# Attention and a state-space layer on one core: two PSUM tiles of three banks around one shared bank

## The chip, the cores and the metric

One core of a Trainium2 chip. The time is that of the device in microseconds, as a median over runs of the whole program.

## What is computed

Two independent layers on a sequence of 2048 rows of 640 values, put side by side in the output. Cut to what matters:

```
# A: a diagonal state-space layer
h = Lam_bar * h + (B_bar x)[t]            # 2048 steps, complex, 640 states
y = 2 * Re(C h) + x * Dskip
# B: attention, 32 query heads of 20 values, one shared key and value head
scores = (q @ k.T) * 20 ** -0.5           # 32 heads, 2048 x 2048
p = softmax(scores); o = p @ v
out = concat([y, o @ wo], axis=-1)
```

## The kernel before

A planner written in Python (`Plan`, and the loop in `main`) places every instruction when the program is built. It keeps a clock for each engine, offers at each step all instructions that could come next, and takes the one that can begin first, with biases. The biases and limits come from a random generator (`vary`), whose seed is changed 64 times over the run; `SEEDS` holds the seeds. So the order on each engine is fixed in the program, and an edit of the planner, or of the seeds, moves instructions everywhere.

Attention is worked in 32 groups (4 blocks of 512 queries x 8 groups of 4 heads). A group has 64 units: one head's 512 queries against 128 keys, which is one PSUM bank of 512 float values on 128 partitions. The 2048 units go one of two ways:

- Most are exponentiated by ScalarE (`ex_op`, line 1263). TensorE fills a tile of two or three banks with QK products (`fill_op`; all products are recorded at line 421), and one ScalarE instruction turns the whole tile into bf16 numbers in `P`.
- The others are VectorE's units, called D here. `dx_op` (line 1269) copies a bank of scores as integers into `Pd`, and `sh_op` (line 1274) makes three shifted copies of up to three units at once; the four together, read as bf16, stand for the exponential. A group may have at most 16 (`QUOTA`), and `want_d` decides whether the next fill takes one along.

TensorE then multiplies both kinds with the values (`pv_op`), up to four products at once in the bank `PV`, and VectorE takes the finished group out (`raw_op`, line 1307).

PSUM has eight banks: tile `R0` with three, tile `R1` with two, `PV`, and two banks `B0` and `B1`. Tiles are filled in turn, `R0`, `R1`, `R0`, and so on, and a tile can be filled again once its exp is done. D units use `B0` or `B1`, or the third bank of `R0` (`R0c`), which is then lent and the tile is filled with two units. The list `owner` says who has a bank.

The background work uses `B0` and `B1` too, one bank for each sum: the Q projections, the state-space layer's input products (`scan_in`; line 901 reads 1024 values out of a bank, each twice), its output products (`y_tile`), and the output projection (`proj_ops`). GpSimd does the products between the scans (line 917). At the end `last_ops` uses the free tiles for the last output rows. Where TensorE would be idle for long, the planner puts in products with zeros (`PV<-cs,VP`) to keep its clock up.

`P` holds 25 units as 10 slots, of three and two in turn.

Of the kernel before, what the change touches and what calls it, by code (L numbers as in the profile page):

```python
# [243 lines left out]
class _Kernel:  # L244
    S, D, H, DH = 2048, 640, 32, 20
    NC, NQB, NKC, NGG = 5, 4, 16, 8
    BANKS = 2
    PIECES = "abcd"
    TILES, PTILES, DUNITS, DSHIFT, QRING = (3, 2), 10, 9, 3, 4
    SHIFTS = (0, 33, 65, 95)  # L250

# [13 lines left out]
    SEEDS = (19006, 20002, 21006, 22006, 23001, 24003, 25001, 26002, 27008, 28003, 0, 30006, 31008, 32005, 33006,  # L265
# [28 lines left out]
    def alloc(self):  # L294
        S, NC = self.S, self.NC
        nc = self.nc
        self.R = [self.scope.enter_context(nc.psum_tensor(f"R{i}", [128, 512 * n], FP32))
                  for i, n in enumerate(self.TILES)]
        self.PV = self.scope.enter_context(nc.psum_tensor("PV", [128, 512], FP32))
        self.BB = self.scope.enter_context(nc.psum_tensor("B", [128, 512 * self.BANKS], FP32))  # L300
        self.B = [self.BB[:, 512 * i:512 * i + 512] for i in range(self.BANKS)] + [self.R[0][:, 1024:1536]]
        self.bkeys = [f"B{i}" for i in range(self.BANKS)] + ["R0c"]
        self.p.psum.update(["R0", "R0c", "R1", "R1b", "PV", *(f"B{i}" for i in range(self.BANKS))])
# [25 lines left out]
        self.sb("P", [128, self.PTILES * 5 // 2, 512], BF16)  # L329
# [7 lines left out]
        self.wq_raw = self.P[:].rearrange("p s n -> p (s n)")[:, 18 * 512:18 * 512 + NC * 640].rearrange("p (c n) -> p c n", c=NC)  # L337
# [92 lines left out]
    def setup(self):  # L430
        t, NC, S = self.t, self.NC, self.S
        self.x_keys = [f"xbT{c}" for c in range(NC)] + [f"xbT{NC - 1}b"]
        K = self
# [48 lines left out]
        pk = ["P7", "P8", "P9"]  # L482
# [23 lines left out]
        banks = [(K.R[1], 0, "R1"), (K.R[1], 512, "R1b"), (K.BB, 0, "B0"), (K.BB, 512, "B1")]  # L506
# [39 lines left out]
        for m, src, keys in ((0, K.R[1][:, 0:1024], ["R1", "R1b"]), (1, K.BB[:, 0:1024], ["B0", "B1"])):  # L546
            dve(lambda e, m=m, src=src: e.tensor_reduce(
                out=K.mabs[:, m:m + 1], in_=src, axis=AX.X, op=ALU.max, apply_absolute_value=True),
                keys, [f"mabs{m}"], n=1024)
# [339 lines left out]
    def scan_in(self, ops, dve, b, c):  # L889
        K, NC, prog = self, self.NC, self.prog  # L890
        u = NC * b + c
        xs = [f"xaT{b % 2}_{i}" for i in range(NC)]
        gate = lambda: prog["u"] >= u and prog["x"] >= b
        for k, (nm, BT) in enumerate((("BTre", K.BTre), ("BTim", K.BTim))):
            h = Hold()
            for cd in range(NC):
                ops.append(self.mms([self.m1(lambda h=h: h.T[:, :], BT[:, cd, 128 * c:128 * c + 128],
                                             K.xaT[:, b % 2, cd, :], cd == 0, cd == NC - 1)],
                                    [f"{nm}{i}" for i in range(NC)] + xs, [None], accum=cd > 0, lock=cd == 0,
                                    gate=gate if cd == 0 else None, hold=h))  # L900
            dve(lambda e, k=k, h=h: e.tensor_tensor(  # L901
                K.tm[:, 2 * k:2 * k + 2, :], bass.AP(tensor=K.BB, offset=512 * int(h.key[1]),
                                                       ap=[[512 * self.BANKS, 128], [0, 2], [1, 512]]),
                K.cs[:, c, :, :], ALU.mult), [None, "cosT", "sinT"], [f"tm{2 * k}", f"tm{2 * k + 1}"], 1024, hold=h,
                free=True, done=(lambda: prog.update(a=u + 1)) if k else None)
# [162 lines left out]
    def last_ops(self, gates, normed):  # L1068

        K, NC = self, self.NC  # L1070
        spots = [(K.R[0], 0, 0, 512, self.TILES[0]), (K.R[1], 1, 0, 512, self.TILES[1]), (K.BB, 2, 0, 512, self.BANKS)]
        keys = [["R0"], ["R1"], ["B0", "B1"], ["R0c", "PV"]]
# [40 lines left out]
    def vary(self, seed):  # L1113
# [10 lines left out]
        self.lend = r.choice((0.5, 1.0))  # L1124
        self.open, self.first = r.choice((0.6, 0.7)), r.choice(("sy", "proj", None))

    def main(self):
# [10 lines left out]
        tile_left = {}  # L1138
# [27 lines left out]
        fins = self.last_ops([lambda: done(0), lambda: done(1), lambda: done() and cur["raw"] == NG and not (any(owner[:2]) or sy or norm or proj),  # L1166
# [3 lines left out]
        owner = ["rest", "rest", None]  # L1170
        rest[-1].done = lambda: owner.__setitem__(slice(0, 2), [None, None])
        holds, since = {}, {}

        def bank(o):

            f = [i for i in range(2) if owner[i] is None]
            if not f:
                return None
            return min(f, key=lambda i: p.begin("pe", (), (f"B{i}",)))
# [6 lines left out]
        def pick(size, with_d):  # L1186

            g = next(i for i in range(NG) if taken[i] < 64)
            out, d = [], None
# [7 lines left out]
            if with_d:  # L1197
                gd = d_group(g)
                j = min(range(4), key=lambda j: (dcount[gd][j], made(gd, j), -len(left[gd][j])))
                if left[gd][j]:  # L1200
                    d = (gd, j)
                    heads.add(j)
# [27 lines left out]
        def want_d(g, t, n_tile, lent=False):  # L1230
            if not (g > 0 or taken[g] >= 24) or d_group(g) is None:
                return False
            if dunit_left.get(cur["d"] - self.DUNITS, 0):
                return False
            if lent:
                return (self.lend < 9 and owner[2] is None and t_left() and backlog(t) <= self.backlog - 0.5 * n_tile - self.lend
                        and p.begin("pe", (), ("R0c",)) <= t + self.spared[n_tile])
            if bank(None) is None:
                return False
            if any(owner[:2]) and any(t - x > self.starved[name] * (name != "qt" or len(self.qsent) > 0) for name, x in since.items()):  # L1240
# [4 lines left out]
        def fill_op(n, out, d, x):  # L1245
            lst, reads, writes = [], set(), ([f"R{n % 2}"] if out else []) + ["R0c"] * (len(out) == 3)
            units = list(out) + ([d] if d else [])
            wide = len({j // 2 for _, j in units}) == len(units)
            for i, (g, j) in enumerate(units):
                kc = left[g][j][-1]  # L1250
                lo, n_rows = (64 * (j // 2), 64) if wide else (32 * j, 32)
                dst = K.B[x][:, :] if i == len(out) else K.R[n % 2][:, 512 * i:512 * i + 512]
# [3 lines left out]
            if d:  # L1256
                writes.append(K.bkeys[x])
            return self.mms(lst, sorted(reads), writes, kind="QK")

        def ex_op(n, size):  # L1260
            b = 5 * (n // 2 % (self.PTILES // 2)) + 3 * (n % 2)
            dst = K.P[:, b:b + size, :].rearrange("p a n -> p (a n)")
            return Op("act", lambda e: e.activation(dst, K.R[n % 2][:, 0:512 * size], ACT.Exp, scale=self.exp_scale),  # L1263
                      [f"R{n % 2}"] + ["R0c"] * (size == 3), [f"P{n % self.PTILES}"], occ=act_t(512 * size), lat=0.17)

        def dx_op(n):
            u, x = n % self.DUNITS, holds[n]
            key = K.bkeys[x]
            return Op("dve", lambda e: e.tensor_scalar(K.Pd[:, 0, u, :], K.B[x][:, :], self.d_off, 0.0, op0=ALU.add,  # L1269
                                                       op1=ALU.max), [key], [f"Pd{u}_0"], occ=dve_t(512))  # L1270
# [14 lines left out]
        def pv_op(g):  # L1285
            lst, keys = [], set()
            for j in range(4):
# [3 lines left out]
                if how == "act":  # L1291
                    rhs, w = K.P[:, b, :], 0
                    keys |= {f"P{a}", "VP0"}
# [18 lines left out]
        while True:  # L1312
# [14 lines left out]
            if cur["fill"] < cur["act"] + 2 and any(x < 64 for x in taken) and not early:  # L1327
                n = cur["fill"]
                g = next(i for i in range(NG) if taken[i] < 64)
                if g in qt_done:  # L1330
                    t = p.begin("pe", (), (f"R{n % 2}",))
                    size, x = self.TILES[n % 2] - (n % 2 == 0 and owner[2] is not None), bank(None)
                    d = want_d(g, t, n % 2)
                    if not d and size == 3 and want_d(g, t, 0, True):
                        size, d, x = 2, True, 2
                    out, d = pick(size, d)
# [5 lines left out]
                    if d is None and want_d(g, t, 2):  # L1342
                        d = pick(0, True)[1]
                        if d:
                            offer("fill", fill_op(n, [], d, bank(None)), 0.2, arg=([], d, bank(None)))
            full = bool(tiles) and tile_left.get(tiles[0][0] - self.PTILES, 0) > 0
            if tiles:
                n, out = tiles[0]
                if tile_left.get(n - self.PTILES, 0) == 0:
# [20 lines left out]
            for name, th in threads:  # L1370
# [15 lines left out]
                if o.eng == "pe":  # L1386
                    bias = 0.0 if own else self.wait - 0.1 * (name == self.first)
                elif own:
# [32 lines left out]
            if kind == "bg":  # L1421
                th = dict(threads)[name]
                th.popleft()
                if o.lock:
                    owner[int(o.hold.key[1])] = name
                    since.pop(name, None)
                if o.free:
# [3 lines left out]
            elif kind == "fill":  # L1431
                out, d, x = arg
                self.units += len(out) + (d is not None)
                if out:
                    n = cur["fill"]
                    cur["fill"] += 1
                    tile_left[n] = len(out)
# [3 lines left out]
                if d:  # L1441
                    g, j = d
# [4 lines left out]
                    holds[cur["d"]] = x  # L1447
                    owner[holds[cur["d"]]] = "D"
                    cur["d"] += 1
            elif kind == "ex":  # L1450
                n, out = tiles.popleft()
                cur["act"] += 1
                b = 5 * (n // 2 % (self.PTILES // 2)) + 3 * (n % 2)
                for i, (g, j, kc) in enumerate(out):
                    items[g][j].append(("act", kc, n % self.PTILES, b + i, n))
            elif kind == "dx":
                n, (g, j, kc) = dunits.popleft()
                owner[holds[n]] = None
                u = n % self.DUNITS
                if half and (u == 0 or half[0][1][0] != g):  # L1460
                    shifts.extend((tuple(half), i) for i in range(1, 4))
                    half.clear()
                half.append((u, (g, j, kc)))
                dunit_left[n] = 4
                items[g][j].append(("dve", kc, u, 0, n))
                if len(half) == self.DSHIFT or u == self.DUNITS - 1:
# [6 lines left out]
            elif kind == "pv":  # L1473
                g = cur["pv"]
                for j in range(4):
                    if items[g][j]:
# [3 lines left out]
                        if how == "act":  # L1480
                            tile_left[h] -= 1
# [49 lines left out]
```

## Time and profile before

| | |
|---|---|
| median of 3 runs | 770.23 us (769.33 to 770.93) |
| profiled execution | 770.28 us |
| its span, first to last instruction | 768.6 us |
| mean granted clock of TensorE | 0.989 |
| busy: ScalarE, VectorE, TensorE, GpSimd | 98%, 92%, 92%, 58% |
| exps (line 1263) | 677 instructions, 733.1 us busy |
| copies of D units (line 1269) | 436 instructions, 295.4 us busy |
| shifted copies (line 1274) | 513 instructions, 260.2 us busy |

The busy time of a group is the time that its engine had one of its instructions in work; the mean length of one can overlap the next. "Idle before" is the time that the engine had nothing in work ahead of these instructions, and what ended it. A line such as L421 is that of a helper that records every product, so products are told apart by their tiles.

### The profile page before, as it was taken

To read this page: it belongs to the slowest core of one execution; us is meant where nothing else is said; L and a number is where in the kernel's file an instruction comes from. 1 tells how busy PE (TensorE), PEld (TensorE's weight loads), DVE (VectorE), ACT (ScalarE), POOL (GpSimd) and SP (SyncE) were. 2 spreads that over 40 slices of the span, in tenths; PEclk is the share of its full clock that TensorE was granted. 3 is DMA by queue.
4 is the path that set the end of the run, shared out by engine and by line. 5 is a ranking of instruction groups with operands and counts; after the bars stand their busy time and mean duration, and the time that the engine had idled before them with its cause. 6 is when DMAs were issued, how large, how long until landed. Compare 5 with 4: busy or idle time off the path is not lost.

```text
span 768.6 us, 16664 instructions
## 1 busy us (share of the span) xinstructions
PE 704.8 (92%) x6538; PEld 213.4 (28%) x6538; DVE 708.3 (92%) x1236; ACT 752.5 (98%) x710; POOL 446.0 (58%) x867
## 2 busy tenths in 40 slices
PE   5799988888889999998889999988889999889998
PEld 2222222222222333322223323322223332223333
DVE  5599999999998999999997999999999789999986
ACT  8999999999999999999999999999999999999995
POOL 5612354579989931088997300199986469990040
PEclk9899999899999999999999999999999999999999
DMA  9366301000021100220002100040000201000020
GB/s 186 57 143 134 74 16 49 8 24 14 3 51 30 42 8 27 56 60 15 15 9 67 42 23 9 23 93 10 15 15 28 66 33 34 14 15 17 18 61 35
DMA packets 61179, 31.50 MB, mean 41 GB/s; under 512 B 41510, under 2 KB 61102, under 8 KB 61102
## 3 DMA queue, kind: packets, MB, share of 16 engines
q1 hardware_dynamic: 59606, 30.14, 15.9%
q8 instruction: 52, 0.85, 0.5%
q10 hardware_dynamic: 1496, 0.30, 0.2%
q14 instruction: 25, 0.20, 0.1%
HBM read 9.21 MB, written 12.69 MB: 28 GB/s over the span
## 4 chain that ended last, share of the span: by engine, by line
ACT 74%; PE 15%; DVE 9%; POOL 1%; DMA 1%; issue 1%; ACTq 0%; DVEq 0%; POOLq 0%
ACT P L1263 72%; PE R L421 5%; PE PV L421 5%; PE B L421 4%; DVE Pd L1274 4%; DVE Pd L1269 3%; DVE hh L928 1%; DVE tm L901 1%; POOL tm L858 1%; DMA WO<-in_B_wk_dram 1%; ACT cs L691 1%; ACT Pd L690 0%; ACT KT L538 0%; DVE CGre L860 0%; ACT L503 0%
## 5 line engine op out<-in xcount | busy, mean ns | idle before, releaser
L1263 ACT ACTIVATE P<-R 128x1024 bf16<-128x1024 f32 (+1 forms) x677 | 733.1, 1354 | 4.3 <-PE R L421 1.8
L421 PE MATMUL R<-QT,KT 32*128 32x512 bf16 (+1 forms) x1685 | 266.9, 389 | 48.6 <-ACT P L1263 37.1
L1269 DVE TENSOR_SCALAR Pd<-B 128x512 int16<-128x512 f32 x363 | 245.5, 682 | 19.4 <-PE B L421 17.0
L1274 DVE TENSOR_SCALAR Pd<-Pd 128x1536 int16<-128x1536 int16 (+2 forms) x513 | 260.2, 541 | 0.4
L421 PE MATMUL PV<-Pd,VP 128*32 128x512 bf16 x1744 | 256.9, 386 | 2.0 <-DVE OTr L1307 1.0
L421 PE MATMUL PV<-P,VP 128*32 128x512 bf16 x1612 | 253.3, 389 | 0.7 <-DVE OTr L1307 0.6
L917 POOL TENSOR_TENSOR tm<-hh,cs 128x128 bf16<-128x128 f32 x320 | 163.9, 533 | 17.7 <-DVE hh L928 8.3
L421 PEld LDWEIGHTS R<-QT,KT 32*128 32x128 bf16 (+1 forms) x1685 | 66.1, 91 | 301.0 <-ACT P L1263 271.0
L421 PE MATMUL B<-QT,KT 32*128 32x512 bf16 x363 | 141.0, 389 | 0.0
L917 POOL TENSOR_TENSOR uh<-tm 128x128 bf16<-128x128 bf16 x160 | 81.0, 527 | 97.6 <-DVE tm L901 93.7
L917 POOL TENSOR_TENSOR W<-tm 128x128 bf16<-128x128 bf16 x160 | 93.5, 608 | 49.4 <-PE B L421 45.3
L421 PEld LDWEIGHTS PV<-Pd,VP 128*32 128x32 bf16 x1744 | 60.1, 94 | 65.7 <-issue 40.5
L421 PEld LDWEIGHTS PV<-P,VP 128*32 128x32 bf16 x1612 | 58.1, 94 | 58.8 <-issue 46.6
L1011 POOL TENSOR_TENSOR OTd<-OTd,rwide 128x128 bf16<-128x128 bf16 x80 | 33.2, 443 | 60.0 <-DMA OTd<-o_rows 58.2
L1269 DVE TENSOR_SCALAR Pd<-R 128x512 int16<-128x512 f32 x73 | 49.9, 683 | 3.0 <-PE R L421 2.4
L901 DVE TENSOR_TENSOR tm<-B,cs 128x1024 bf16<-128x1024 f32 x40 | 48.5, 1213 | 1.0 <-PE B L421 0.6
L858 POOL TENSOR_SCALAR tm<-W,sc 128x128 f32<-128x128 bf16 x40 | 32.3, 821 | 27.5 <-DVE CGre L860 15.9
L421 PE MATMUL B<-CGre,W 128*128 128x384 bf16 (+1 forms) x160 | 46.4, 305 | 0.0
L421 PE MATMUL B<-CGim,W 128*128 128x384 bf16 (+1 forms) x160 | 45.5, 299 | 0.0
L928 DVE TENSOR_TENSOR_SCAN hh<-sc,hini,uh 128x512 f32<-128x512 f32 x30 | 40.7, 1358 | 0.0
L421 PEld LDWEIGHTS B<-QT,KT 32*128 32x128 bf16 x363 | 32.9, 91 | 0.0
L421 PE MATMUL B<-xaT,BTre 128*128 128x512 bf16 x100 | 30.1, 384 | 0.1
(149 smaller groups left out, 437.2 us busy)
## 6 DMA issues: line engine op xcount, KB each, us to landing
o_rows<-OTr SPq DMA_DIRECT2D x32, 128.0 KB, 1.7
QT<-q_rows SPq DMA_DIRECT2D x30, 128.0 KB, 2.2
q_rows<-Qd SPq DMA_DIRECT2D x16, 160.0 KB, 2.9
OTd<-o_rows SPq DMA_DIRECT2D x16, 160.0 KB, 3.4
out_dram<-ystage SPq DMA_DIRECT2D x16, 160.0 KB, 1.9
out_dram<-ostage SPq DMA_DIRECT2D x12, 160.0 KB, 1.8
P<-in_B_wq_dram SPq DMA_DIRECT2D x1, 800.0 KB, 5.6
WO<-in_B_wo_dram SPq DMA_DIRECT2D x4, 200.0 KB, 3.4
```

The costliest lines, as they stand in the source:

```text
L421: ins = e.matmul(o() if callable(o) else o, lhsT=l, rhs=r, start=st, stop=sp, skip_group_check=True, **kw)
L691: act(lambda e, c=c, b=b: e.activation(K.cs[:, c, :, :].rearrange("p i n -> p (i n)"), K.tri[:, 4 * b + 2:4 * b + 4, :].rearrange("p r n - ...
L858: pool(lambda e, y=y, c=c, gy=gy, i=i: e.tensor_scalar(K.ctmp[:, i:i + 128], y[:, i:i + 128], sc[:, gy, c:c + 1], None, op0=ALU.mult), key ...
L901: dve(lambda e, k=k, h=h: e.tensor_tensor(K.tm[:, 2 * k:2 * k + 2, :], bass.AP(tensor=K.BB, offset=512 * int(h.key[1]), ap=[[512 * self.BA ...
L917: put(lambda e, c0=c0, end=end: e.tensor_tensor(out[:, c0:end], a[:, c0:end], b[:, c0:end], op), reads, [writes + h], n, gate=None if i el ...
L928: dve(lambda e, ri=ri, ini=ini: e.tensor_tensor_scan(K.hh[:, ri, :], dec, K.uh[:, ri, :], ini, ALU.mult, ALU.add), ["sc", *(f"uh{ri}{h}" f ...
L1011: ops.append(Op("pool", lambda e, c=c, m=m: e.tensor_tensor(K.OTd[:, m, c], K.OTd[:, m, c], K.rwide[:, c], ALU.mult), rw + [f"OTe{dd}" for ...
L1263: return Op("act", lambda e: e.activation(dst, K.R[n % 2][:, 0:512 * size], ACT.Exp, scale=self.exp_scale), [f"R{n % 2}"] + ["R0c"] * (siz ...
L1269: return Op("dve", lambda e: e.tensor_scalar(K.Pd[:, 0, u, :], K.B[x][:, :], self.d_off, 0.0, op0=ALU.add, op1=ALU.max), [key], [f"Pd{u}_0 ...
L1274: return Op("dve", lambda e: e.tensor_scalar(K.Pd[:, i, a:b, :], K.Pd[:, 0, a:b, :], float(self.SHIFTS[i]), 0.0, op0=ALU.subtract, op1=ALU ...
```

## The change

PSUM is cut anew: one tensor `R` of seven banks and `PV`. Tile 0 has banks 0 to 2, bank 3 is the one shared bank `B0`, tile 1 has banks 4 to 6. Either tile can now hold three units, or two and lend its third bank to a D unit: tile 0 lends bank 2, tile 1 bank 4. Both are neighbours of the shared bank. A fill may take two D units along, one in the lent bank and one in the shared bank, and `dx_op` then copies both with one instruction of 1024 values. Background work has the one shared bank where it had two. `P` becomes a ring of 25 single units. `vary` draws some more limits (`prefer`, `pair`, `more`, `gap`), and all seeds are other ones. Cut to its core:

```diff
-    BANKS = 2
+    BANKS = 1
-    TILES, PTILES, DUNITS, DSHIFT, QRING = (3, 2), 10, 9, 3, 4
+    TILE, PUNITS, DUNITS, DSHIFT, QRING = 3, 25, 9, 3, 4
...
-        self.B = [self.BB[:, 512 * i:512 * i + 512] for i in range(self.BANKS)] + [self.R[0][:, 1024:1536]]
+        self.RB = self.scope.enter_context(nc.psum_tensor("R", [128, 512 * (2 * self.TILE + 1)], FP32))
+        self.R = [self.RB[:, 0:1536], self.RB[:, 2048:3584]]
+        self.B = [self.RB[:, a:a + 512] for a in (1536, 1024, 2048)]
+        self.bkeys = ["B0", "R0c", "R1c"]
...
+        self.lend, self.prefer = r.choice((0.0, 0.5, 1.0)), r.choice((False, True))
+        self.pair, self.more = r.choice((True, True, False)), r.choice((0.0, 0.5, 1.0))
+        self.gap = dict(sy=r.choice((0.0, 4.0, 8.0)), proj=r.choice((0.0, 4.0, 8.0)), sa=r.choice((0.0, 0.0, 4.0)),
+                        qt=r.choice((0.0, 0.0, 4.0)))
...
-            f = [i for i in range(2) if owner[i] is None]
...
+            return 0 if owner[0] is None else None
...
         def dx_op(n):
             u, x = n % self.DUNITS, holds[n]
+            if n in pairs:
+                a = 1024 if x == 1 else 1536
+                return Op("dve", lambda e: e.tensor_scalar(K.Pd[:, 0, u:u + 2, :].rearrange("p u n -> p (u n)"), K.RB[:, a:a + 1024],
+                                                           self.d_off, 0.0, op0=ALU.add, op1=ALU.max),
...
-                    size, x = self.TILES[n % 2] - (n % 2 == 0 and owner[2] is not None), bank(None)
-                    d = want_d(g, t, n % 2)
-                    if not d and size == 3 and want_d(g, t, 0, True):
-                        size, d, x = 2, True, 2
+                    lent = 1 + n % 2
+                    size, x = self.TILE - (owner[lent] is not None), [0]
+                    if self.pair and size == 3 and want_d(g, t, 0, lent, True):
+                        size, d, x = 2, 2, [lent, 0] if lent == 1 else [0, lent]
+                    elif (d := want_d(g, t, n % 2)) and not (self.prefer and size == 3 and want_d(g, t, 0, lent)):
+                        d = 1
+                    elif size == 3 and want_d(g, t, 0, lent):
+                        size, d, x = 2, 1, [lent]
```

In the changed kernel the exp stands at line 1276, the copies of D units at lines 1283 and 1286, and the shifted copies follow behind.

151 lines of the change are left out of this document (81 added, 70 removed), and 8 rows, old and new, of the table SEEDS.

## The prediction

> **What bounds the kernel now.** I read the page first: the busy times, then the chain that ended last.
>
> ```profile
> span 768.6 us, 16664 instructions
> ...
> PE 704.8 (92%) x6538; PEld 213.4 (28%) x6538; DVE 708.3 (92%) x1236; ACT 752.5 (98%) x710; POOL 446.0 (58%) x867
> ...
> ACT 74%; PE 15%; DVE 9%; POOL 1%; DMA 1%; issue 1%; ACTq 0%; DVEq 0%; POOLq 0%
> ```
>
> ScalarE is busy 98% and carries 74% of the chain, nearly all of it in the exps of line 1263. Next I read the groups of instructions with shapes kept apart, since the change alters shapes.
>
> ```profile
> L1263 ACT ACTIVATE P<-R 128x1024 bf16<-128x1024 f32 x419 | 457.8, 1189 | 1.1 <-PE R L421 0.7 <-PE B L421 0.2
> L1263 ACT ACTIVATE P<-R 128x1536 bf16<-128x1536 f32 x258 | 418.3, 1621 | 3.2 <-PE R L421 1.2 <-PE B L421 1.1 <-PE PV L421 0.6
> ...
> L1269 DVE TENSOR_SCALAR Pd<-B 128x512 int16<-128x512 f32 x363 | 245.5, 682 | 19.4 <-PE B L421 17.0
> L1274 DVE TENSOR_SCALAR Pd<-Pd 128x1536 int16<-128x1536 int16 x354 | 205.5, 608 | 0.2
> ...
> L901 DVE TENSOR_TENSOR tm<-B,cs 128x1024 bf16<-128x1024 f32 x40 | 48.5, 1213 | 1.0 <-PE B L421 0.6
> ```
>
> There are 677 exps over 419 x 2 + 258 x 3 = 1612 units. The idle column is almost empty, but it misleads: neighbouring exps overlap in the records (457.8 + 418.3 is more than the span), so an exp that starts late looks merely long or short, not preceded by idle time. The starts in the timeline tell more. Where the next tile was ready, starts follow each other after 0.904 us (two banks) or 1.331 us (three banks), medians over the whole run. So a bank costs 0.427 us and an instruction 0.904 - 2 x 0.427 = 0.050 us. At these spacings the exps need 419 x 0.904 + 258 x 1.331 = 722.2 us. From the first start (21.7) to the last end (759.0) they take 737.4. The other 15 us are starts that came late: 14.8 us between starts, 0.3 us in the last exp's own end. Summed by what was running before the late start: after a two-bank exp 12.4 us over 418 (29.6 ns each), after a three-bank exp 2.4 us over 258 (9.4 ns each). A longer exp gives TensorE more time to bring the next tile.
>
> How a late start looks, in the timeline (start, length):
>
> ```profile
> 485.06 2.15 ACT L1263 ACTIVATE P<-R 128x1024 bf16<-128x1024 f32 x2
> ...
> 486.69 0.33 PE L421 MATMUL B<-CGim,W 128*128 128x384 bf16 x1
> 486.70 0.69 DVE L1307 CAST OTr<-PV 128x512 bf16<-128x512 f32 x1 [0.19 <-PE PV L421]
> 486.95 0.39 PE L421 MATMUL R<-QT,KT 32*128 32x512 bf16 x3
> ...
> 487.38 1.02 ACT L1263 ACTIVATE P<-R 128x1024 bf16<-128x1024 f32 x1 [0.17 <-PE R L421]
> ```
>
> TensorE had other products in its order, so the fill came at 486.95 and the exp started 0.43 us after it. Last, the waits and the clock (columns of the second: length, busy us of PE, PEld, DVE, ACT, POOL with counts, PEclk, DMA).
>
> ```profile
> DVE Pd L1269 <- PE B L421: 17.0, 58, 0.7
> ...
> PE R L421 <- DVE Pd L1269: 3.2, 8, 0.8
> ```
>
> ```profile
> 28.00:35.00 7.00, 6.59 (x29) 1.21 (x29) 1.55 (x4) 6.38 (x7) 2.31 (x11) 0.52 0.05 4
> ...
> 141.00:147.00 6.00, 5.97 (x36) 1.12 (x32) 5.17 (x11) 5.33 (x5) 2.42 (x4) 0.50 0.08 26
> ```
>
> TensorE's fills hardly ever wait for VectorE's copies (3.2 us in 8 waits); by the same list they wait for ScalarE 598 times, 271 us. In three short stretches, 17 us in all, the clock is about half: the two shown and 120 to 124 (0.57, ScalarE busy throughout). ScalarE idles 0.62 + 0 + 0.67 = 1.3 us in them.
>
> **The change, part by part.** The counts are those of the instructions in the two built programs; everything else keeps its count.
>
> Exps: 419 -> 387 of two banks, 258 -> 279 of three. That is 11 instructions and one unit less: 387 x 0.904 + 279 x 1.331 = 721.2 us, so **-1.0 us**, all on the bounding engine. [...]
>
> VectorE's units: 436 -> 437. As instructions: 436 -> 391 copies of one bank and 0 -> 23 of two. One bank is spaced at 0.601 us. No copy of two banks is in the trace; the nearest is line 901, also 1024 float values from PSUM, spaced at 1.134. From below it could cost 2 x 0.427 as a pure stream on ScalarE's rate, from above 2 x 0.601. I take 1.134: 23 x 1.134 - 45 x 0.601 = 26.1 - 27.0 = -1.0 us. The shifted copies (1274): +15 of three units (0.469), -30 of two (0.336), -30 of one (0.21), +12 of four, not in the trace (0.60 by the steps of 0.133): 7.0 - 10.1 - 6.3 + 7.2 = -2.1 us. Together -3.1 us of VectorE. This is not on ScalarE's path by itself. In 6 of 15 stretches of 50 us VectorE is busy over 48 us; if its saving is spread evenly, 1.2 us fall there. ScalarE's idle there is small, so I count half: **-0.6 us** (bounds 0 and -3.1).
>
> TensorE: 677 -> 666 fills (0.32 us from the start of one to the next product, read at 102.64) and 881 -> 866 groups of PV products (0.22 us), 3 more warming products: about -6 us of 582. It waits for ScalarE in most fills, so this is worth nothing by itself.
>
> Where the units go is the real change. Before, 363 of VectorE's 436 units lay in the two banks of their own and 73 in the lent third bank of tile 0. After, 365 lie in lent banks of either tile and 72 in the shared bank. So tile 1 gets a third bank, and 574 of 666 fills are three units (318 of 677 before). Late starts, priced by what covers them: 387 x 29.6 + 278 x 9.4 = 14.1 us against 14.8, so **-0.7 us**. This is the price I take, because it follows the mechanism seen in the starts. Two other prices of the same term are rivals below.
>
> Background work now has one bank, where it had two. While VectorE reads that bank, TensorE cannot begin the next background sum, and what is queued behind it on TensorE waits too, if the order puts it too early. I cost it at nothing: VectorE's own units leave the shared bank (363 -> 72), and in the new order the last y products stand at unit 1982 of 2048, before at 2002, so background work doesn't pile up at the end. Without that cover one late background read is 1.2 us (line 901).
>
> Set-up and tail: the same instructions on other banks. First exp at 21.7 and the 9.6 us after the last exp are kept, cost 0; the last fill has 18 PV products behind it where it had 30, but the tail follows the last exp's end. The P ring keeps 25 units, now without holes; exps waited for none, so 0. DMAs and the queues of SP and POOL keep their counts.
>
> Sum: -1.0 - 0.7 - 0.6 = -2.3 us. The profiled execution took 770.28 (span 768.6 and 1.7 around it), the median of the three runs is 770.23. So 768.0. A measurement here can tell 0.2%, 1.5 us, from no change: below 768.7 is faster, above 771.8 slower.
>
> **Rivals.**
>
> No change. Late starts go with the size of the fill before them, not with the cover: per fill of two units 8.9 ns, of three 24.3, of four 29.7. The new mix (21, 574, 71) gives 16.2 us, +1.4, which eats the 1.0 of the exps: 770.7, or 770.1 with VectorE's relief. For it: a fill of three waits for one more bank. Against: size and place go together in this trace.
>
> Slower: the lent bank ties three engines. In the new order 378 fills write a bank that VectorE's copy of two fills earlier has to have left (235 before, 68 of them a lent bank with its unit); if VectorE is late, the whole tile is late and ScalarE with it. Fills that reused a lent bank so soon were followed by 31.5 ns of lateness each, the rest by 19.6, and the 16 that reused a bank after one fill by 92. With 378 x 31.5 + 288 x 19.6 = 17.5 us the exps lose 2.7 more: 770.3 - 1.0 + 2.7 = 772.0. It decides against the change above 27 ns per lent fill (0.378 x 27 + 5.6 = 14.8 + 1.0), and reaches 774 at 37. Against it: before, banks were lent when the others were full, so those fills were late for that reason too.
>
> The pairs are rare and the change does little: 46 of 437 units. That alone is 23 x 0.068 = 1.6 us of VectorE, none of it seen: 770.2, same.
>
> The clock. If TensorE idles a little in every round of the banks, its clock drops more often than three times. Ten more stretches like those three would be 57 us, with 1.3/17 lost in each us: +4.3, so 772.3. [...]
>
> **How the numbers follow.** Forecast 0.46, no change 0.20 and rare pairs 0.04, lent bank 0.24, clock 0.06. So faster 0.46, same 0.24, slower 0.30. The forecast's own range is 765.0 to 768.7: its low end lets half of the late starts fall to the three-bank price ((14.8 - 6.3)/2 = 4.3, and 1.0). The range of 8 in 10 goes from 765.0 to 773.0, over the rivals at 770, 772.0 and 772.3 and part of the lent bank's upper end.
>
> **What would show it.** Right: 387 and 279 exps at the old spacings; the exps' time from first start to last end 735.1; VectorE's pair of banks near 1.13 from start to start; TensorE waiting for line 1286 (the copies) no more than a few us. Wrong: a wait of PE R for VectorE's copies grown from 3.2 towards 10 us with late starts behind it, more than three dips of the clock, or late starts above 17 us in sum.

## The result: slower by 0.3%

The changed kernel takes 771.65 us (median of 20 runs, 770.50 to 776.97), the kernel before 769.80 beside it (20 runs): a ratio of 1.0032 [1.0018, 1.0046]. Timed once more, beside other runs of the kernel before, it was 1.0025 [1.0011, 1.0039]. So it loses 1.9 to 2.5 us where the prediction had it gain 2.3; the forecast was wrong in sign. By the marks that the prediction set from 770.2 (faster below 768.7, slower above 771.8) 771.65 by itself would be no change, and it lies in the range of 8 in 10 (765.0 to 773.0), though outside the forecast's own (765.0 to 768.7). That it is slower shows in the ratio, whose interval leaves out 1.

The profiled execution of the changed kernel took 773.31 us, 1.7 above its own median, so single places of it are not typical; a second profile of the same kernel (772.58 us) and a second one of the kernel before (769.35 us) are read beside it. The second of after is slow too, 1.4 above the median of its own series (771.22).

The page of after (first profile), the lines that answer to those of before:

```profile
span 771.5 us, 16592 instructions
...
PE 683.8 (89%) x6479; PEld 213.3 (28%) x6544; DVE 710.7 (92%) x1181; ACT 751.5 (97%) x699; POOL 446.6 (58%) x867
...
ACT 81%; PE 8%; DVE 6%; SPq 3%; DMA 2%; issue 1%; ACTq 0%
```

The span grew by 2.9 us while ScalarE is busy 1.0 us less (752.5 before). In the chain one entry is new, SyncE's queue (`SPq`) with 3%, and DMA has 2% where it had 1%. The groups with shapes kept apart:

```profile
L1276 ACT ACTIVATE P<-R 128x1536 bf16<-128x1536 f32 x279 | 411.6, 1627 | 3.6 <-PE R L421 2.2 <-issue 1.3
L1276 ACT ACTIVATE P<-R 128x1024 bf16<-128x1024 f32 x387 | 394.8, 1181 | 4.5 <-PE R L421 4.2
L1286 DVE TENSOR_SCALAR Pd<-R 128x512 int16<-128x512 f32 x391 | 263.7, 684 | 24.4 <-PE R L421 21.5
...
L901 DVE TENSOR_TENSOR tm<-R,cs 128x1024 bf16<-128x1024 f32 x40 | 48.5, 1213 | 1.3 <-PE R L421 1.2
...
L1283 DVE TENSOR_SCALAR Pd<-R 128x1024 int16<-128x1024 f32 x23 | 28.0, 1219 | 2.7 <-PE R L421 2.4
```

The exps number 387 and 279, as foreseen, but their idle column is 8.1 us where it was 4.3: that is the first sign of late starts. Measured start to start, an exp that found its tile ready still costs 0.904 and 1.330 us. The 23 copies of a pair take 1.22 us each, as line 901 does, which was the row they were priced by; start to start it is 1.140 us, priced at 1.134. The waits:

```profile
PE R L421 <- ACT P L1276: 53.2, 158, 1.0
DVE Pd L1286 <- PE R L421: 21.5, 50, 1.9
...
PEld R L421 <- DVE Pd L1286: 7.3, 24, 0.4
...
ACT P L1276 <- PE R L421: 6.3, 10, 1.3
...
PE R L421 <- DVE Pd L1286: 4.4, 17, 0.9
...
PE R L421 <- DMA BTre<-in_A_B_re_dram: 1.9, 1, 1.9
```

TensorE's products wait 4.4 us for VectorE's copies (3.2 before, and 2.2 in the second profile of after), its weight loads 7.3 us in 24 short waits, where before had 9.6 us in 36 for `B0` and `B1`. So these waits did not grow. The last line is new: before had no wait of a product for `BTre`.

Late starts (start of the next exp less 0.904, 1.331 or, for one bank, 0.477 us), summed by time in us, for profiles of both kernels and of two that are told of below. "Tail" is from the last exp's end to the span's end:

| kernel | span | 0-80 | 80-200 | 200-400 | 400-600 | 600 on | sum | tail |
|---|---|---|---|---|---|---|---|---|
| before | 768.6 | 2.9 | 2.6 | 3.8 | 3.1 | 2.4 | 14.8 | 9.5 |
| before, second | 767.6 | 2.6 | 2.1 | 3.9 | 3.2 | 2.5 | 14.3 | 9.5 |
| after | 771.5 | 6.0 | 1.4 | 5.1 | 3.1 | 2.5 | 18.1 | 10.0 |
| after, second | 770.8 | 4.0 | 3.1 | 5.2 | 3.1 | 2.5 | 17.8 | 10.0 |
| loads reordered | 768.5 | 3.6 | 1.4 | 5.3 | 2.9 | 2.5 | 15.7 | 10.1 |
| the same, second | 769.7 | 4.1 | 1.9 | 5.4 | 2.9 | 2.5 | 16.8 | 10.1 |

Means of two profiles each: late starts +3.4 us (17.95 against 14.6), tail +0.5, exps -1.0, and the first exp starts 0.1 later. That is +3.0, and the spans differ by 3.05. So the books close: the gain on the exps came, and about a dozen late starts and the tail took more. Of the 3.4 us, 2.25 lie in the first 80 us and 1.3 between 200 and 400. These are two executions slower than most; the medians differ by 1.9 to 2.5 us, so up to about one us of the 3.05 belongs to what went wrong in these two alone.

Where single moves were tried, the whole list of planned instructions was placed a second time in an edited order, so that everything else kept its place; line numbers there are some 21 higher. Ratios are to the kernel before, run beside them.

### The profile page after: what moved, and what is told of

Same layout as the page of the kernel before. It is cut to its first block, busy times and chain, and to the rows that moved or that the text cites. A ratio compares the mean times of both kernels' runs of the same rounds, so it can differ in the third digit from the quotient of the medians.

```text
span 771.5 us, 16592 instructions
## 1 busy us (share of the span) xinstructions
PE 683.8 (89%) x6479; PEld 213.3 (28%) x6544; DVE 710.7 (92%) x1181; ACT 751.5 (97%) x699; POOL 446.6 (58%) x867
## 4 chain that ended last, share of the span: by engine, by line
ACT 81%; PE 8%; DVE 6%; SPq 3%; DMA 2%; issue 1%; ACTq 0%
ACT P L1276 79%; PE R L421 5%; PE PV L421 3%; SPq L402 2%; DVE Pd L1291 2%; DVE Pd L1286 2%; DVE hh L928 1%; DMA o_rows<-OTr 1%; ACT cs L691 1%; SPq L404 1%; DVE tm L901 0%; DMA BTre<-in_A_B_re_dram 0%; ACT Pd L690 0%; DMA WO<-in_A_Lambda_im_dram 0%; DVE ystage L962 0%
## 5 line engine op out<-in xcount | busy, mean ns | idle before, releaser
L421 PE MATMUL R<-QT,KT 32*128 32x512 bf16 (+1 forms) x2048 | 262.2, 387 | 63.4 <-ACT P L1276 53.2
L1286 DVE TENSOR_SCALAR Pd<-R 128x512 int16<-128x512 f32 x391 | 263.7, 684 | 24.4 <-PE R L421 21.5
L1291 DVE TENSOR_SCALAR Pd<-Pd 128x1536 int16<-128x1536 int16 (+3 forms) x480 | 260.8, 579 | 0.4
L901 DVE TENSOR_TENSOR tm<-R,cs 128x1024 bf16<-128x1024 f32 x40 | 48.5, 1213 | 1.3 <-PE R L421 1.2
L421 PE MATMUL R<-CGre,W 128*128 128x384 bf16 (+1 forms) x160 | 46.4, 305 | 0.1
L421 PE MATMUL R<-CGim,W 128*128 128x384 bf16 (+1 forms) x160 | 45.5, 300 | 0.0
L421 PE MATMUL R<-WO,OTd 128*128 128x320 bf16 x160 | 30.4, 302 | 0.4 <-DVE Pd L1286 0.2
L421 PE MATMUL R<-xaT,BTre 128*128 128x512 bf16 x89 | 27.4, 384 | 3.6 <-DMA BTre<-in_A_B_re_dram 1.9
L1283 DVE TENSOR_SCALAR Pd<-R 128x1024 int16<-128x1024 f32 x23 | 28.0, 1219 | 2.7 <-PE R L421 2.4
L421 PE MATMUL R<-xaT,BTim 128*128 128x512 bf16 x88 | 26.5, 383 | 1.8 <-DVE Pd L1286 0.8
```

The lines of the kernel that those rows point to most:

```text
L421: ins = e.matmul(o() if callable(o) else o, lhsT=l, rhs=r, start=st, stop=sp, skip_group_check=True, **kw)
L901: dve(lambda e, k=k, h=h: e.tensor_tensor(K.tm[:, 2 * k:2 * k + 2, :], bass.AP(tensor=K.RB, offset=1536, ap=[[3584, 128], [0, 2], [1, 512] ...
L1283: return Op("dve", lambda e: e.tensor_scalar(K.Pd[:, 0, u:u + 2, :].rearrange("p u n -> p (u n)"), K.RB[:, a:a + 1024], self.d_off, 0.0, o ...
L1291: return Op("dve", lambda e: e.tensor_scalar(K.Pd[:, i, a:b, :], K.Pd[:, 0, a:b, :], float(self.SHIFTS[i]), 0.0, op0=ALU.subtract, op1=ALU ...
```

## The early late starts: loads, Q products, the clock

At 55 us in the first profile of after (timeline; start, length):

```profile
51.77 1.27 SPq L402 DMA_TRANSPOSE BTim<-in_A_B_im_dram  x1
...
53.09 1.89 SPq L404 DMA_DIRECT2D WO<-in_B_wo_dram  x3
...
54.26 0.59 PE L421 MATMUL R<-xaT,BTre 128*128 128x512 bf16 x2 [1.93 <-DMA BTre<-in_A_B_re_dram]
...
54.79 0.39 PE L421 MATMUL R<-QT,KT 32*128 32x512 bf16 x3
```

SyncE issues five transposing loads of `BTre` and five of `BTim` by turns, 1.27 us each but for one of 1.88. The fifth `BTre` was issued at 50.46 and had landed at 53.85. The first product that reads it stands in the new order at unit 78 of 2048, in the old at unit 86, and the fill behind it waits with it: the exp started 1.45 us late. Then the clock fell to half from 56.0 to 59.4 (0.50 granted), and three more were 0.30, 0.19 and 0.89 late.

The other early place is fill 7, at 32 us, with the clock at half (0.50 granted from 22.0 to 32.2):

```profile
28.70 0.61 PE L421 MATMUL R<-QT,KT 32*128 32x512 bf16 x3 [0.73 <-ACT P L1276]
...
29.64 1.91 PE L421 MATMUL R<-xbT,wq 128*128 128x512 bf16 x4 [0.33 <-issue]
...
31.49 0.89 PE L421 MATMUL R<-QT,KT 32*128 32x512 bf16 x6
```

The five products of a Q projection stand in one row between fills 6 and 7 (the records show four), and the exp of fill 7 started 1.44 us late. In before they are spread over fills 7 to 10.

Theory A: these two places carry the loss. Rival B: the lent bank couples VectorE to ScalarE everywhere. The loads reordered, five `BTre` ahead of five `BTim` in the same ten places of SyncE's order:

```diff
+bt = [i for i, x in enumerate(log) if x is a load of BTre or BTim]
+for i, x in zip(bt, sorted((log[i] for i in bt), key=is_BTim)):
+    log[i] = x
```

> The changed kernel with one edit: SyncE issues the five transposed loads of BTre ahead of the five of BTim, where they took turns. All other engines keep their instructions and order. Theory A (the extra time arose before 80 us, where the order puts work ahead of its data): the first product with BTre no longer waits near 52 us; the late start of 1.45 us of exp 27 goes, and of the 1.4 us of late starts at exps 28 to 30 behind the clock's fall to half at 56 us most goes too: 1.4 to 2.9 us less than the changed kernel, ratio to the kernel before 0.9995 to 1.0014. Theory B (the lent banks tie VectorE to the tiles through the whole run): no change, ratio 1.0032.

1.0012 [1.0002, 1.0023]. The late starts at exps 27 to 30 are gone and the chain of waits has no SyncE queue. Next, the two places apart and together: fills 7 and 8 put between the Q products, and both edits.

```diff
-fill 6, Q x5, fills 7 and 8
+fill 6, Q x2, fill 7, Q x2, fill 8, Q x1
```

> The changed kernel with one edit: the five products of the Q projection that stand in a row ahead of fill 7 (at half clock, 0.43 us each) are put apart, two before fill 7, two before fill 8, one behind it. Theory A: exp 7 was late by 1.44 us; three of the five no longer stand before it, so about 1.0 us less, ratio to the kernel before about 1.0019. If the clock falls elsewhere in other executions the gain is smaller. Theory B: no change, 1.0032.

> Both edits of the two runs before it. Theory A: the sums add: 2.4 to 3.9 us less than the changed kernel, ratio to the kernel before 0.998 to 1.000; late starts up to 80 us about 2.5 us, as in the kernel before (2.9), instead of 6.0. Theory B: 1.0032.

1.0028 [1.0017, 1.0038] and 1.0025 [1.0013, 1.0037]. Exp 7 was no longer late, but exps 9 and 10 were, by 2.02 and 0.61 us (1.26 and 0.61 with both edits): the work ahead of fill 9 at half clock (0.50 granted from 24.8 to 35.0 in the first of the two) is the same. The gains did not add: of the 2.4 to 3.9 us that theory A expected from both edits some 0.5 came, so these two places by themselves do not carry the loss.

The changed kernel and the reordered loads had not run beside each other, so both were timed once more, on one chip:

> The changed kernel itself, unchanged, on the same chip as the next one. So far the reordered loads (1.0012) were compared with the changed kernel (1.0032) over different chips, and a kernel with the old order of loads showed no wait for BTre in its own profile. If the wait for BTre is part of the loss: near 1.003, with a late exp near 55 us in most executions. If 1.0032 was a matter of chips: near 1.0012 here as well.

> The changed kernel with the five loads of BTre issued ahead of those of BTim, again, beside the unchanged one. If the wait for BTre is part of the loss: 1.0 to 2.0 us below the unchanged one on this chip, that is a ratio smaller by 0.0013 to 0.0026. If it is not: the same within 0.0010.

1.0025 [1.0011, 1.0039] and 1.0015 [1.0004, 1.0026]: 0.8 us apart, with intervals that overlap: short of what was expected if the wait counts (0.0013 to 0.0026), at the edge of what was expected if it doesn't (0.0010). And the second profile of the unchanged after shows no wait at all for `BTre`:

```profile
51.11 1.88 SPq L404 DMA_DIRECT2D WO<-in_B_wo_dram  x3
...
52.76 0.13 PEld L421 LDWEIGHTS R<-xaT,BTre 128*128 128x128 bf16 x2 [0.56 <-issue]
52.79 0.59 PE L421 MATMUL R<-xaT,BTre 128*128 128x512 bf16 x2
```

Here SyncE's queue ran 2.0 us earlier (`WO` issued at 51.11, not 53.09; the transposes behind each other from 30.15, not 32.40). Before has the same spread (31.55 in its first profile) and no wait, because its first product came at 55.15. So the wait is real, and it belongs to executions whose queue runs late: of four profiles with the new order and the old loads two have it (1.9 and 1.1 us), of eight with the loads reordered none. Its mean price lies between nothing and some 1.5 us; more than that isn't settled.

The clock was tried by warming it: 16 products with no use put ahead of and between the first fills, fill 2 moved one place ahead, with the loads reordered; the same edit in the kernel before, and the kernel before by itself.

> The kernel before once more, for a second profile and a bound on the comparison: ratio 1.000. Its first profile had half clock at 28 to 35, 120 to 124 and 141 to 148 us. If these falls belong to the kernel's order they stand at the same places again; if they belong to the execution they move, and the late starts that go with them (1.6 us from 141 to 148) come or go.

> The changed kernel with the loads reordered as in the first run, and in the set-up 16 warming products (6 before the row scale product near 20 us, 3, 3 and 4 before fills 4, 5 and 6, into banks that are free there) and fill 2 ahead of the last of four groups of V products. Theory A (the set-up's slow stretch at half clock, 22 to 32 us, costs the late starts of exps 2 and 7, 1.06 and 1.44 us): the clock stays up, exp 7 is late by 0.5 at most, exp 2 by 0.5; 1.5 us less than with the loads alone, ratio to the kernel before 0.9993. If the clock falls all the same: no gain, 1.0012.

> The kernel before with the same 16 warming products and fill 2 moved. If the slow stretch in the set-up costs the kernel before as much as its profile shows (exps 2, 9, 10 late by 0.69, 0.13, 0.74 us): 0.8 to 1.2 us less, ratio 0.9985 to 0.999. If its clock mostly holds there anyway: 0.9995 to 1.

1.0007 [0.9991, 1.0023], 1.0043 [1.0019, 1.0066] and 1.0008 [0.9993, 1.0023]. In the changed kernel exps 2 and 7 were then in time (exp 4 was 0.84 us late instead), and yet it got slower. The timeline of its profiled execution shows one reason:

```profile
70.05 1.14 SPq L423 DMA_TRANSPOSE W<-in_A_C_re_dram  x1
...
71.20 0.39 PE L442 MATMUL R<-QT,KT 32*128 32x512 bf16 x3 [3.68 <-DMA QT<-q_rows]
...
71.64 1.02 ACT L1297 ACTIVATE P<-R 128x1024 bf16<-128x1024 f32 x1 [3.34 <-PE R L442]
```

A fill waited 3.68 us for another load, `QT`, and right behind that gap the clock fell (71.6 to 75.0; 0.54 granted over 71.9 to 75.3). Again a load that the fixed order left too little time, in this execution at least: no other profile of a kernel with the picked seeds shows more than 0.4 us of this wait. Whether it is what made the other executions slower isn't shown. In the kernel before, warming brought nothing that can be measured.

## The middle: VectorE's copies at the end of a group

Of the 5.1 us between 200 and 400 us, three starts carry 3.15: at 282 (1.13), 349 (0.88) and 351 (1.14). Without these three the stretch has 2.0 us, where before has 3.8 with its own largest ones. VectorE's timeline of after around two of them:

```profile
343.04 1.21 DVE L901 TENSOR_TENSOR tm<-R,cs 128x1024 bf16<-128x1024 f32 x1
344.17 5.45 DVE L1291 TENSOR_SCALAR Pd<-Pd 128x1536 int16<-128x1536 int16 x8
349.54 1.28 DVE L1286 TENSOR_SCALAR Pd<-R 128x512 int16<-128x512 f32 x2
```

A group ends there. Eight shifted copies in a row (5.45 us) stand ahead of two copies, one of them out of a lent bank, and the tile with that bank is filled only at 350.65. Two attempts to move the order: the fills at 349 and 698 us put earlier, and then VectorE's copies out of the lent banks as well.

```diff
-PV, PV, PV, fill 293      # and fill 609, two places
+fill 293, PV, PV, PV
```

> The changed kernel with the loads reordered, and two fills moved ahead of products that wait or are not urgent: fill 293 (exp late by 0.88 us at 349 us, behind PV products that wait for VectorE's shifted copies) and fill 609 (late by 0.42 at 698 us, behind y products). If these late starts are accidents of order: 0.9 to 1.3 us less than with the loads alone, ratio to the kernel before 1.000. If VectorE is the bound there (the copies out of lent banks late too): exp 294, late by 1.14, becomes later by what 293 gains, and only 0.4 us is left: 1.0007.

```diff
+move(copy of the lent bank at 282 us, 2 places ahead in VectorE's order)
+move(copy of the lent bank at 349 us, 3 places ahead in VectorE's order)
+move(fills 230, 293, 294: 4, 3 and 5 places ahead in TensorE's order)
```

> The changed kernel with the loads reordered, and at two places VectorE's copy of the lent bank of tile 0 taken earlier: at 282 us ahead of the 1.2 us read of the shared bank, at 349 us ahead of three of eight shifted copies; the fills 230, 293 and 294 that wait for these copies stand ahead of the PV products that followed them in time. If the late starts there (1.13, 0.88 and 1.14 us) are the lent bank's coupling, VectorE's order behind it: they go, 2 to 3 us less than with the loads alone, ratio to the kernel before 0.997 to 0.999. If the lateness is TensorE's own load of PV products, it comes back within the next fills: 0 to 1 us less, 1.000 to 1.0012.

1.0019 [1.0007, 1.0031] and 1.0020 [1.0011, 1.0030], both with the loads reordered, so no better than that alone (1.0012, 1.0015). The lateness came back in the next fills: 2.02 us at exp 294 in the first; 0.61 and 0.50 at exps 231 and 232, and 0.38, 0.91 and 0.28 at 294 to 296 in the second. So it is not one copy in the wrong place that makes these starts late. That VectorE and TensorE are behind with a group's end fits, but no run shows it by itself.

Rival B was tested where it would show most. If a lent bank ties ScalarE to VectorE, slower copies must hurt the changed kernel more. Each copy of one bank was made as two halves of 256 values (by estimate 0.068 us more each, 2 x 0.601 - 1.134): 436 copies in before, 391 in after with the loads reordered.

```diff
-e.tensor_scalar(Pd[:, 0, u, :], bank, ...)
+for i in (0, 256):
+    e.tensor_scalar(Pd[:, 0, u, i:i + 256], bank[:, i:i + 256], ...)
```

> The kernel before, every one of its 436 one-bank copies made as two of half a bank, in the same place: VectorE works 436 x 0.068 = 30 us more, nothing else changes. VectorE was busy over 48 of 50 us in 6 of 15 stretches, so some of it must show: between 12 and 25 us more. To be read against the next run.

> The changed kernel with the loads reordered, its 391 one-bank copies made as two of half a bank: VectorE works 391 x 0.068 = 26.6 us more. Theory B (the lent banks pass VectorE's lateness on to ScalarE more readily than banks of its own): it loses more per us of added work than the kernel before, over 1.2 times as much. Theory A (no such difference): the same share, within a fifth.

1.0059 [1.0044, 1.0074] and 1.0063 [1.0046, 1.0080]. In the traces a half is followed by the next instruction after 0.331 us, so a copy in halves costs 2 x 0.331 - 0.601 = 0.061 us more: 26.6 us of VectorE in before and 23.9 in after. Before lost 0.0059 x 769 = 4.5 us (12 to 25 had been expected), 17% of that; after lost 0.0063 - 0.0012 = 0.0051, 3.9 us, 16%. The intervals leave 3.4 to 5.7 us for the one and 2.4 to 5.5 for the other, so a difference by a third isn't ruled out; but no stronger coupling shows, and B has lost its support as a general cause. The pairs by themselves, each of the 23 made as two copies of one bank:

> The changed kernel, each of the 23 copies of a pair of banks replaced by two copies of one bank, in the same place, the order of all else kept. Price of the pair: VectorE works 23 x 0.068 = 1.6 us more. Theory A: VectorE is not on ScalarE's path, so 0 to 0.4 us more, ratio 1.0032 to 1.0037. Theory C (the pair matters): 1.6 us more, ratio 1.005.

1.0025 [1.0011, 1.0038], where the pairs in one piece gave 1.0025 and 1.0032: nothing that can be measured. At a sixth, 23 x 0.068 = 1.6 us of VectorE would be 0.3 us.

## The tail

Behind the last fill of after the last background sum, five products of `WO,OTd`, stands between the last PV groups (VectorE had read the one shared bank out at 759.76, just behind the last fill at 759.71), and ten more such products run ahead of the column sums (`E,OTr`), where before has eight. TensorE's timeline of after:

```profile
761.22 0.85 PE L421 MATMUL R<-WO,OTd 128*128 128x320 bf16 x5
762.00 0.39 PE L421 MATMUL PV<-P,VP 128*32 128x512 bf16 x2
762.33 1.53 PE L421 MATMUL R<-WO,OTd 128*128 128x320 bf16 x10
763.69 0.24 PE L421 MATMUL R<-E,OTr 128*128 128x4 bf16 x4
```

The timeline of the kernel before at the same place:

```profile
759.11 0.58 PE L421 MATMUL PV<-P,VP 128*32 128x512 bf16 x2
759.33 0.38 PE L421 MATMUL PV<-Pd,VP 128*32 128x512 bf16 x1
759.64 1.26 PE L421 MATMUL R<-WO,OTd 128*128 128x320 bf16 x8
760.74 0.24 PE L421 MATMUL B<-E,OTr 128*128 128x4 bf16 x4
```

The column sums come 2.25 us after the last exp's end (761.44) instead of 1.70 (759.04): 0.55 us, as much as the tail grew. The five products put right behind the last fill, and eight instead of ten ahead of the sums, on top of the last kernel's moves:

```diff
-last fill, PV x16, WO,OTd x5, PV x2, WO,OTd x10, E,OTr
+last fill, WO,OTd x5, PV x18, WO,OTd x8, E,OTr, WO,OTd x2
```

> As the first of these four, and in the tail the five products of the last background sum that has to wait for the one shared bank stand ahead of the last PV products, where they stood between them, and the four column sums ahead of the last two of ten output products. The time from the last exp to the end is 9.97 us with the loads reordered and 9.35 in the kernel before. If the shared bank's order makes this difference: 0.3 to 0.6 us less than the first of these four.

1.0012 [0.9997, 1.0028], 0.6 us below the run before it by the ratios and 0.1 by the medians (770.10 and 770.01). The sums came 1.87 us after the last exp's end, but the tail was 9.95 us still, 0.1 less: the two products put behind the sums now stand ahead of the next ones that are needed (`ident,rden`), which came 1.28 us behind the sums instead of 1.01. So the place of the sums alone doesn't make the tail. Of the versions of the new layout this one and the reordered loads are the fastest, and neither beats the kernel before.

## The layout without its picked seeds

The seeds choose the order, and the change replaced them all. Theory L: the new layout is the weaker one, and the new seeds hide most of that. Rival S: the layout is good, its list of seeds is at fault, and with other seeds it is the faster one. Both kernels were run with all seeds 0 and with seeds 1 to 64. The same number doesn't draw the same limits in the two, since `vary` draws more of them after the change. With seed 0 the new planner puts a new sum of the output projection off by up to 8 us behind the last one and one of the Q projections by up to 4 (`gap`), which the old planner can't do. So these runs compare layout and planner together.

```diff
-SEEDS = (4007, 5002, 6006, ...)
+SEEDS = (0,) * 64          # or tuple(range(1, 65))
```

> The kernel before with all 64 seeds set to 0, so that the planner draws one set of limits throughout and orders everything anew. Its exps need 726.7 us at the old spacings (448 of two banks, 241 of three, 2 of one), 4.5 more than with its own seeds. Late starts are what the seeds were to lower: I expect 5 to 15 us more than the kernel before, ratio 1.006 to 1.02. To be read against the next run.

> The changed kernel with all 64 seeds set to 0. Its exps need 716.3 us (385, 276, 2), 10.4 less than those of the run before it. Theory S (the layout is good, and what went wrong lies in the orders that this list of seeds draws): it is faster than the run before it, by up to 10 us. Theory L (the layout itself makes more late starts, whatever the order): late starts grow by about as much as the exps shrink, and the two are equal or this one slower.

> The kernel before with the seeds 1 to 64. Its exps need 728.5 us. As with zeros: ratio 1.006 to 1.025.

> The changed kernel with the seeds 1 to 64. Its exps need 722.4 us, 6.1 less than those of the run before it. Theory S: faster than the run before it, by 3 to 6 us. Theory L: equal or slower.

| seeds | before | after |
|---|---|---|
| all 0 | 1.0273 [1.0219, 1.0327] | 1.0910 [1.0865, 1.0954] |
| 1 to 64 | 1.0340 [1.0302, 1.0379] | 1.0634 [1.0595, 1.0672] |

With seeds that nobody picked the new layout is behind by 6% and 3%, so rival S falls for these seeds. (The old layout lost more than was expected, too.) The exps themselves need less in both cases (716.3 against 726.7 us, 722.4 against 728.5 at the old spacings). With seeds 1 to 64 the late starts are 58.7 us against 25.2. With zeros they are 36.0 against 26.6, and the exps end at 773.8, before those of the old layout (775.0); but then 66 us follow. After the last fill 40 of the 160 products of `CGre` for y, 20 of the 80 for the skip term, 5 of the 100 of `BTre` and 40 of the 160 of `WO,OTd` in the output projection are left; in the old layout 30 of these last and none of the others. The timeline of after with seeds 0 and a wait of its list:

```profile
812.98 0.48 PE L417 MATMUL R<-CGre,W 128*128 128x384 bf16 x1 [18.42 <-POOL W L913]
```

```profile
ACT W L1097 <- PE R L417: 61.7, 2, 61.3
```

At 813 us, 39 us after the last exp, TensorE has waited 18.4 us for GpSimd to finish the scan's output (and ScalarE, by the second line, stands idle for 61.3 us between the last exp and its read of the last rows), the end of a chain (input product, VectorE, scan, GpSimd, output product) that is long and was started too late. The scan's input sums were a quarter, half, three quarters and wholly done at units 550, 1107, 1555 and 2048, in the old layout at 523, 912, 1285 and 1652: one bank, not two, fed them. That fits theory L, though the bank and the planner's new limits were not told apart.

With seeds 1 to 64 the loss has another form. The scan's input sums are early (units 422, 888, 1441 and 1783, in the old layout 508, 979, 1448 and 1874), less is left behind the last fill (12 products of `CGre` against 25), and the exps are late on the way:

```profile
ACT P L1272 <- PE R L417: 27.2, 42, 8.2
...
ACT P L1272 <- PE PV L417: 15.1, 7, 3.1
```

The longest wait ends at 78.74 us: ahead of it, from 70.8 us on, TensorE does nothing but background sums, all in the one bank, and idles 0.65, 1.00 and 0.95 us between them until VectorE is done; the fill then waits 0.81 us for the load of its queries. The second line is exps that wait for room in `P` (3.1 us in the old layout). Up to the last exp the clock is at half for 89 us, in the old layout for 44.

The picked seeds avoid the first form (the last y products stand at unit 1982). That the tail and orders that run closer to their loads are what stays of it is argued, not shown.

## Why the prediction was wrong, point by point

- **Exps, -1.0**: right. 387 and 279 at 0.904 and 1.330.
- **Late starts, -0.7**: the step that failed; it measured +3.4 (17.95 against 14.6). The prices by cover, 29.6 and 9.4 ns, were means over the whole run. After 80 us the kernel before has 27.0 behind a two-bank exp and 6.8 behind a three-bank one; after has 31.6 and 3.4 in its first profile, 35.3 and 5.2 in its second. So three-bank exps covered more, as foreseen, and two-bank ones less. And the price was spread evenly over all fills, while the time sits in single places: 1.4 us at fill 7, up to 2.8 at the load of `BTre` and the clock's fall behind it, 3.15 in three starts at a group's end. What stands ahead of these fills could be read in the order before the run; that the queue would run late and where the clock would fall could not. Of the three signs of being wrong that were named, only this one came, late starts above 17 us; the exps took 739.7 and 739.4 us from first start to last end, where 735.1 was to show the forecast right.
- **Set-up and tail, cost 0**: wrong. "The same instructions on other banks" looked at counts and not at what stands ahead of what. The first 80 us are worth +2.25 (in the late starts above), the tail +0.5. That the DMAs keep their counts was true and beside the point: the product moved against its load.
- **VectorE's relief, -0.6**: not borne out. VectorE is busy 710.7 and 709.1 us in the two profiles of after, 708.3 and 709.1 in those of before, so the 3.1 us less did not come. The copies went as priced; but a shifted copy of three units, with no idle time behind it, is followed by the next instruction after 0.546 us in the mean where it was 0.530, and on 369 of them that is 5.7 us. Why is open. That a sixth of 3.1, by the runs with the halved copies, would have been 0.5 is luck: half of what falls in busy stretches was a guess between 0 and 3.1.
- **Background on one bank, at nothing**: the cover named for it (last y products at unit 1982) did hold in the kernel as built, and it is the seeds' work. With seeds that nobody picked, layout and planner together cost 3% to 6%, and even with the picked ones the last background sum stands in the tail, since its bank came free only behind the last fill.
- **No change by fill size** (16.2 us of late starts): fell short by 1.75.
- **The lent bank** had the nearest time (772.0) and late starts (17.5), though by another way than it said. Its price was 31.5 ns for each lent fill, and it decides above 27; after 80 us the profile shows 21.4 ns over 324 of them and 17.5 over the other fills, the second profile 22.6 and 22.4, and where VectorE was slowed both kernels lost about the same share. Its mechanism is there in three starts, where VectorE is behind at a group's end.
- **The clock** as a rival is not borne out: falls before the tail were two in each profile of after, and three and two in those of before. They last 3.4, 6.8 or 10.2 us, in the first profiles at 0.50 granted: 28.2 to 35.0, 120.4 to 123.8 and 140.9 to 147.7 us in before, 22.0 to 32.2 and 56.0 to 59.4 in after. In the 3.4 us ahead of these five TensorE was busy 0.88, 1.93, 2.01, 1.73 and 1.74 us, so each had idle time of TensorE ahead of it, as the rival supposed; but as little (1.73 in before from 18.0 to 21.4, 1.95 in after from 166.0 to 169.4) had no fall behind it elsewhere, and the new order had no more falls than the old. What sets their length and place is not shown; the falls of one and the same kernel stand elsewhere in another execution, in before at 28.2, 120.4 and 140.9 us, then at 23.3 and 122.2. A fall still costs where it comes: behind the one at 166.8 us in the second profile of after (10.2 us long) two exps are 0.90 and 0.46 us late, which the first profile doesn't have.

## What to carry to other kernels

A late start has an address: before an average price is put on all tiles, list the products that stand directly behind a load, a row of background products or a group's end in the new order, and compare their distance to what they wait for with that of the old order. A product that moves eight units ahead of 2048 can outrun its load, and in some executions only, so one profile isn't enough to price it. When a change also picks new seeds, run both layouts with seeds that were not picked: that shows how much of the time the picking holds up, here 3% to 6% the other way, for layout and planner together.

## What the runs showed of the hardware

- SyncE's queue of loads ran up to 2.25 us earlier or later from one execution of a kernel to the next (the five transposes of x from 30.15 or from 32.40 us).
- Filling a half-clock stretch with 16 products that do no work brought nothing that can be measured: 1.0008 [0.9993, 1.0023] in the kernel before, though the clock then didn't fall until 121 us in its profile (mean granted 0.997, against 0.989 and 0.991 in the two profiles without them).
- With VectorE at 92% busy and ScalarE the bound, about a sixth of what is put on VectorE comes back as the kernel's time: 4.5 of 26.6 us and 3.9 of 23.9.
